# Where seven tiles begin in SBUF: the forms of x moved to seven places modulo 128 bytes

## The chip, the core and the metric

The kernel runs on one core of a Trainium2 chip. The metric is the device time of one execution in microseconds, lower is better. Three runs of the kernel before gave 974.46, 974.54 and 976.66 us (median 974.54 us).

## What is computed

The reference is attention with a block-causal mask over 4 batches, 8 heads, 576 positions and head size 64, followed by two layers of `x @ w_in`, a pointwise function, `@ w_out`, over 2304 tokens, with model width 512 and inner width 2048:

```python
attn = softmax(where(block_i >= block_j, q @ k.T / 8, -1e9)) ; x = attn @ v   # -> [2304, 512]
h = x @ w_in ; x = (h * cos(h)) @ w_out        # first layer
h = x @ w_in ; x = (max(h, 0) ** 2) @ w_out    # second layer, the output
```

All is float32. Each large product is made of three products of parts: a value is split into a high part that TensorE takes exactly in its fp32r format and a low part that is the rest, and `mm3` adds high·high, high·low and low·high in PSUM.

## The kernel before, in words

The order of the work on every engine is written out by a planner (`Recorder.schedule`) before the program is made. It works with costs, due times and data dependences of operations and knows nothing of addresses, so a change of addresses leaves its order as it is.

The first 400 us or so are attention and the first half of the first layer. The change touches what follows: three stages (`for stage in range(3)`, the second half of the first layer, and the two halves of the second one). Each stage goes over five groups of tokens (four of 512, one of 256). For a group of 512, x is cut into four quarters, and from these seven forms x0 to x6 are made: four quarters or sums of them, and three more sums, as in Strassen's scheme for 2x2 blocks (Winograd's variant). The seven forms of a half of `w_in` stand beside them in tiles named `w`, and `quad` multiplies form i of w with form i of x, in the order 0, 1, 5, 4, 6, 2, 3. One such product (`product`) is 12 matmuls: 2 halves of the output by 2 of the depth by the three of `mm3`. The weight part is the stationary operand (128 x 128, loaded by an LDWEIGHTS of its own), the part of x is the moving one, 256 columns wide. For the group of 256 tokens, `two` takes forms 0 and 1, then 0 and 4, 12 matmuls each. With two calls for each group and three stages, the matmuls into `h` that move a form of x are 24 x 12 = 288 for each form, plus 144 for x0 and 72 each for x1 and x4: 432 + 360 + 360 + 4 x 288 = 2304.

In the trace the matmul `h<-x,w` moves x and loads w; the buffer numbers are left out of names, so that all seven forms are called x. The LDWEIGHTS for the next matmul runs while a matmul moves its columns.

A form's tile is written by a copy of the high part (L472 on ScalarE) and a subtraction for the low part (L490 on VectorE) in the first two stages. In the second they are also sent to HBM (`xp_d<-x`), and in the third they are read back from there (`x<-xp_d`). In the third stage the product with `w_out` is done in seven forms too (`out_quad`, matmuls into `y`, 256 columns, the moving operand is a form of the weights, the stationary one a form of g). There the fourteen tiles of weight forms sit where room is: two in `raw` tiles, two in the `x` tiles (those that hold unsplit x in the earlier stages), one in `so` tiles, nine in `w` tiles.

**Where tiles begin.** A pool is a stretch of each partition of SBUF, taken in steps of 32 bytes, from the low end or (`side="right"`) from the high end, and its tiles follow each other in the order of their first use. From the sizes of pools and of the fill-in tiles between them (`shim`), counted in bytes modulo 128, the beginnings before the change are: all `w` tiles 0, in both of their pools; all of x, x0 to x6, and the `raw`, `so`, `g`, `c`, `t`, `n`, `ws` and `t0` to `t3` tiles 64. Parts inside a tile begin 512 or 1024 bytes or multiples of it further on, so each operand of a matmul begins where its tile does, modulo 128. A column is 4 bytes in each partition.

Of the kernel before, what the change touches and what calls it, by code (L numbers as in the profile page):

```python
# [11 lines left out]
F32R = mybir.dt.float32r  # L12
# [6 lines left out]
PSUM = bass.MemoryType.PSUM  # L19
# [37 lines left out]
class View:  # L57
    def __init__(self, vt, chain, ix, halves):
        self.vt, self.chain, self.ix, self.halves = vt, chain, ix, halves
# [34 lines left out]


class VTile(View):
    def __init__(self, pool, shape, dtype, tag, bufs, whole=False):
        self.pool, self.shape, self.dtype, self.tag, self.bufs = pool, shape, dtype, tag, bufs
        self.whole = whole
        n = int(np.prod(shape[1:]))  # L100
        self.grain = 32 if n >= 32 else 1
        self.full = (1 << (2 * (n // self.grain + 1))) - 1
        self.real = None
        self.users = []
        self.bank = self.banks = self.before = None
        super().__init__(self, [], np.arange(n).reshape(shape[1:]), 3)

    def alloc(self):
        if self.real is None:
            tag = self.tag if self.bank is None else f"bank{self.bank}"  # L110
            self.real = self.pool().tile(self.shape, self.dtype, tag=tag, name=self.tag, bufs=self.bufs)


class Banks:
# [30 lines left out]
class Recorder:  # L145
# [20 lines left out]
        self.kind = None  # L166
        self.phase = 0

    def tile(self, pool, shape, dtype, tag, bufs=1, whole=False):
        return VTile(pool, shape, dtype, tag, bufs, whole)  # L170

    @contextmanager
    def of(self, kind):
# [208 lines left out]
def kernel(  # L382
# [25 lines left out]
    R = Recorder()  # L408
# [172 lines left out]
    class Pool:  # L581


        def __init__(self, name, **kw):
            self.name, self.kw, self.pool, self.after, self.stack = name, kw, None, (), None
# [18 lines left out]
    def later(names, **kw):  # L604
        return [Pool(n, **kw) for n in names]
# [32 lines left out]
    xs_p, tmp = opened(s1, "xs1", "tmp1")  # L638
    (sb,) = opened(att, "att", side="right")

    def T(pool, shape, dtype, tag, bufs=1):
        return R.tile(pool, shape, dtype, tag, bufs, whole=pool.kw.get("space") == PSUM)

    x_d = T(dram, [KD, 128, NT], F32, "x_d")
    y1_d = T(dram, [KD, 128, NT], F32, "y1_d")
    y_d = T(dram, [KD, 128, NT], F32, "y_d")


# [27 lines left out]
    for i in range(2):  # L676
# [3 lines left out]
        whole = T(sb, [128, 128], F32, f"whole{i}")  # L680
# [585 lines left out]
    for group, steps in WORK:  # L1266
# [12 lines left out]
        if group == (3, 1):  # L1279
            wo_p, x3_p = later(("wo", "x3"), side="right")  # L1280
# [16 lines left out]
        return raw  # L1297

    def x_tile(j):
        return T(x3_p, [128, 2, 2, 256], F32R, f"x{j}")  # L1300

    def x_parts(forms, keep):

        ops = {}
        for j, x in forms:
            t = x_tile(j)
            hi, lo = t[:, 0], t[:, 1]
            hi_part(hi, x)
            lo_part(lo, x, hi)
            if keep is not None:  # L1310
                dma(keep[j], f(t).rearrange("p j k c -> p (j k c)"), 524288)
            ops[j] = hi, lo
        return ops

    @of("forms")
    def kept_parts(keep, which):

        ops = {}
        for j in which:
            t = x_tile(j)  # L1320
            dma(f(t).rearrange("p j k c -> p (j k c)"), keep[j], 524288)
            ops[j] = t[:, 0], t[:, 1]
        return ops
# [319 lines left out]
```

## Time and profile before

| | |
|---|---|
| median of three runs | 974.54 us |
| the profiled execution | 974.84 us, of it 973.0 us from its first to its last instruction |
| TensorE busy (matmuls) | 951.8 us, 98% of the span |
| VectorE, ScalarE, GpSimd busy | 713.8, 602.3, 208.3 us |
| matmuls `h<-x,w`, 128 x 256 | 2304 |

A busy time of TensorE is a union of intervals that overlap, since a matmul begins before the one before it has ended (one takes 276 ns from its first column to its last result, and begins some 115 ns after the one before). What a matmul costs is therefore read from the starts: the time from the start of one row to the start of the next in the timeline, divided by the matmuls in the row.

### The profile page before, as it was taken

To read this page: it belongs to the slowest core of one execution; us is meant where nothing else is said; L and a number is where in the kernel's file an instruction comes from. 1 tells how busy PE (TensorE), PEld (TensorE's weight loads), DVE (VectorE), ACT (ScalarE), POOL (GpSimd) and SP (SyncE) were. 2 spreads that over 40 slices of the span, in tenths; PEclk is the share of its full clock that TensorE was granted. 3 is DMA by queue.
4 is the path that set the end of the run, shared out by engine and by line. 5 is a ranking of instruction groups with operands and counts; after the bars stand their busy time and mean duration, and the time that the engine had idled before them with its cause. 6 is when DMAs were issued, how large, how long until landed. Compare 5 with 4: busy or idle time off the path is not lost.

```text
span 973.0 us, 19283 instructions
## 1 busy us (share of the span) xinstructions
PE 951.8 (98%) x6996; PEld 856.1 (88%) x6996; DVE 713.8 (73%) x1581; ACT 602.3 (62%) x1285; POOL 208.3 (21%) x313
## 2 busy tenths in 40 slices
PE   7979999999999999999999999999999999999998
PEld 5757987889898989999989889998898899999998
DVE  5898667687877455588879797987885737659565
ACT  5787588785889575484758476767564433324222
POOL 3554243447687781000000000000000000000000
PEclk8999999999999999999999999999999999999999
DMA  6755233355656347563355899796947779535321
GB/s 184 192 150 124 67 85 84 105 153 182 176 174 206 109 134 263 200 254 93 109 173 181 317 360 327 268 352 215 358 139 240 245 256 416 194 104 195 96 73 60
DMA packets 155150, 185.29 MB, mean 190 GB/s; under 512 B 71728, under 2 KB 119856, under 8 KB 155056
## 3 DMA queue, kind: packets, MB, share of 16 engines
q1 hardware_dynamic: 155056, 184.07, 57.5%
q8 instruction: 55, 0.90, 0.4%
q14 instruction: 39, 0.32, 0.1%
HBM read 114.29 MB, written 69.73 MB: 189 GB/s over the span
## 4 chain that ended last, share of the span: by engine, by line
PE 88%; DMA 5%; DVE 3%; ACT 2%; issue 1%; POOL 1%; SPq 0%; ACTq 0%; POOLq 0%; DVEq 0%
PE y L548 37%; PE h L548 34%; PE t L566 6%; PE a L558 5%; PE s L558 4%; DMA wi_d<-so 2%; PE s L548 1%; DMA x<-xp_d 1%; DMA w<-wf_d 1%; DMA x<-x_d 1%; DVE e L1046 1%; POOL e L531 0%; DVE c L449 0%; DVE c L748 0%; DVE so L490 0%
## 5 line engine op out<-in xcount | busy, mean ns | idle before, releaser
L548 PE MATMUL h<-x,w 128*128 128x256 f32 x2304 | 315.8, 278 | 1.7 <-DVE r L442 0.9
L548 PEld LDWEIGHTS h<-x,w 128*128 128x128 f32 x2304 | 294.4, 188 | 6.5 <-DVE r L442 1.7
L548 PE MATMUL y<-gh,w 128*128 128x256 f32 (+2 forms) x832 | 214.7, 329 | 7.3 <-POOL w L467 6.6
L548 PEld LDWEIGHTS y<-gh,w 128*128 128x128 f32 x832 | 144.3, 189 | 19.0 <-POOL w L467 7.6
L548 PE MATMUL y<-gl,w 128*128 128x256 f32 (+2 forms) x416 | 135.0, 328 | 0.0
L548 PE MATMUL y<-w,gh 128*128 128x512 f32 (+1 forms) x450 | 124.0, 354 | 0.4 <-DVE gh L490 0.4
L548 PEld LDWEIGHTS y<-w,gh 128*128 128x128 f32 x450 | 78.9, 188 | 12.6 <-DVE gh L490 0.6
L433 ACT ACTIVATE e<-e,st 128x256 f32<-128x256 f32 (+4 forms) x144 | 82.9, 577 | 8.6 <-DVE st L1046 6.9
L1046 DVE CUSTOM_DVE_ANT_0 e<-s,mask 128x128 f32<-128x128 f32 (+4 forms) x160 | 71.3, 478 | 22.9 <-PE s L558 15.3
L531 POOL TENSOR_SCALAR e<-e,st 128x256 f32<-128x256 f32 (+4 forms) x116 | 73.0, 640 | 63.0 <-DVE st L1067 37.0
L548 PEld LDWEIGHTS y<-gl,w 128*128 128x128 f32 x416 | 78.5, 189 | 6.2 <-issue 0.8
L548 PE MATMUL y<-w,gl 128*128 128x256 f32 (+1 forms) x306 | 83.5, 333 | 0.0
L472 ACT ACTIVATE gh<-r 128x512 fp32r<-128x512 f32 (+1 forms) x85 | 51.3, 610 | 40.0 <-DVE r L1404 18.2
L566 PE MATMUL t<-ident,e 128*128 128x128 f32 (+1 forms) x400 | 65.1, 282 | 4.6 <-DVE e L535 2.3
L490 DVE TENSOR_TENSOR gl<-r,gh 128x512 fp32r<-128x512 f32 (+1 forms) x83 | 54.7, 664 | 15.3 <-ACT gh L472 12.4
L442 DVE TENSOR_TENSOR o<-y,o 128x512 f32<-128x512 f32 (+1 forms) x55 | 34.8, 635 | 40.2 <-PE y L548 39.1
L548 PE MATMUL h<-xs2h,w 128*128 128x320 f32 x256 | 62.0, 313 | 0.0
L566 PEld LDWEIGHTS t<-ident,e 128*128 128x128 f32 (+1 forms) x400 | 46.4, 141 | 13.8 <-POOL e L531 4.7
L501 ACT ACTIVATE r<-t 128x384 f32<-128x384 f32 (+1 forms) x95 | 49.2, 531 | 14.6 <-PE t L566 13.1
L433 ACT ACTIVATE t<-raw,minus 128x512 int32<-128x512 int8 x64 | 48.8, 762 | 14.8 <-DMA raw<-in_moe_w_out_dram 6.8
L548 PEld LDWEIGHTS y<-w,gl 128*128 128x128 f32 x306 | 50.2, 188 | 6.1
L548 PE MATMUL h<-xs1h,w 128*128 128x256 f32 x256 | 53.5, 290 | 1.2 <-POOL w L467 0.7
(172 smaller groups left out, 1838.0 us busy)
## 6 DMA issues: line engine op xcount, KB each, us to landing
wi_d<-so SPq DMA_DIRECT2D x84, 256.0 KB, 2.8
w<-wi_d SPq DMA_DIRECT2D x42, 512.0 KB, 6.3
raw<-in_moe_w_in_dram SPq DMA_DIRECT2D x32, 512.0 KB, 4.6
raw<-in_moe_w_out_dram SPq DMA_DIRECT2D x32, 512.0 KB, 4.4
xp_d<-x SPq DMA_DIRECT2D x24, 512.0 KB, 6.0
x<-xp_d SPq DMA_DIRECT2D x24, 512.0 KB, 5.7
y_d<-o SPq DMA_DIRECT2D x34, 256.0 KB, 2.6
o<-y_d SPq DMA_DIRECT2D x32, 256.0 KB, 3.8
```

Source lines behind the costliest of these rows:

```text
L433: return nc.scalar.activation(real(out), real(in_), func, **kw)
L442: out.size / 0.96 + 68, lambda: nc.vector.tensor_tensor(real(out), real(a), real(b), op=op), [out], [a, b],
L472: "ACT": ("ACT", n / 1.2 + 92, lambda: nc.scalar.activation(real(hi), real(x), ACTF.Copy)),
L490: lambda: nc.vector.tensor_tensor(real(lo), real(x), real(f(hi)), op=ALU.subtract), 1,
L501: "ACT": ("ACT", n / 1.2 + 50, lambda: nc.scalar.activation(real(out), real(ps), ACTF.Copy)),
L531: lambda: nc.gpsimd.tensor_scalar(real(out), real(x), real(s), 1.0, op0=ALU.mult, op1=ALU.mult),
L548: lambda: nc.tensor.matmul(real(ps), lhsT=real(lhsT), rhs=real(rhs), start=start, stop=stop, skip_group_check=True),
L558: nc.tensor.matmul(real(ps), lhsT=real(l), rhs=real(r), start=start, stop=stop, skip_group_check=True)
L566: lambda: nc.tensor.transpose(real(out), real(in_), real(ident)[0:rows, 0:rows]), [out], [in_, ident],
L1046: lambda: nc.vector.tensor_tensor_reduce(out=real(e), in0=real(ps), in1=real(m), scale=-1.0, scalar=BIG, op0=ALU.add, op1=ALU.min, accum_o ...
```

## The change

A tile can be asked to lie in a larger slot, some elements behind its beginning. The seven tiles x0 to x6 (4096 bytes for each partition) get slots of 1032 elements, 4128 bytes, so that the beginnings step on by 32 bytes from one to the next, and x3, x5 and x6 begin 4 elements (16 bytes) behind their slot's beginning. The slots follow in the order of first use: x0, x1, x2, x4, x5, x6, x3. The pool grows by 7 x 32 = 224 bytes towards lower addresses, so that its two `x` tiles move as well. Nothing is issued more, less or in another order.

Beginnings modulo 128 bytes:

| tile | x0 | x1 | x2 | x3 | x4 | x5 | x6 | the two `x` tiles | `w` |
|---|---|---|---|---|---|---|---|---|---|
| before | 64 | 64 | 64 | 64 | 64 | 64 | 64 | 64 | 0 |
| after | 96 | 0 | 32 | 48 | 64 | 112 | 16 | 96 | 0 |

```diff
 class VTile(View):
-    def __init__(self, pool, shape, dtype, tag, bufs, whole=False):
+    def __init__(self, pool, shape, dtype, tag, bufs, whole=False, at=0, slot=0):
...
     def alloc(self):
         if self.real is None:
             tag = self.tag if self.bank is None else f"bank{self.bank}"
-            self.real = self.pool().tile(self.shape, self.dtype, tag=tag, name=self.tag, bufs=self.bufs)
+            if not self.slot_size:
+                self.real = self.pool().tile(self.shape, self.dtype, tag=tag, name=self.tag, bufs=self.bufs)
+                return
+
+            t = self.pool().tile([self.shape[0], self.slot_size], self.dtype, tag=tag, name=self.tag, bufs=self.bufs)
+            t = t[:, self.at:self.at + int(np.prod(self.shape[1:]))]
+            names = "abc"[:len(self.shape) - 1]
+            sizes = dict(zip(names, self.shape[1:]))
+            self.real = t.rearrange(f"p ({' '.join(names)}) -> p {' '.join(names)}", **sizes) if len(names) > 1 else t
...
     def x_tile(j):
-        return T(x3_p, [128, 2, 2, 256], F32R, f"x{j}")
+        return T(x3_p, [128, 2, 2, 256], F32R, f"x{j}", at=4 * (j in (3, 5, 6)), slot=1032)
```

## Rows read from the trace of the kernel before

**Rows 1.** The page: busy time of engines, the clock, and the chain's shares.
```profile
PE 951.8 (98%) x6996; PEld 856.1 (88%) x6996; DVE 713.8 (73%) x1581; ACT 602.3 (62%) x1285; POOL 208.3 (21%) x313
...
PEclk8999999999999999999999999999999999999999
...
PE 88%; DMA 5%; DVE 3%; ACT 2%; issue 1%; POOL 1%; SPq 0%; ACTq 0%; POOLq 0%; DVEq 0%
PE y L548 37%; PE h L548 34%; PE t L566 6%; PE a L558 5%; PE s L558 4%; DMA wi_d<-so 2%; PE s L548 1%; DMA x<-xp_d 1%; DMA w<-wf_d 1%; DMA x<-x_d 1%; DVE e L1046 1%; POOL e L531 0%; DVE c L449 0%; DVE c L748 0%; DVE so L490 0%
```

**Rows 2.** Waits of PE from 405 to 960 us: total, times, longest.
```profile
PE h L548 <- DVE r L442: 0.9, 2, 0.6
PE h L548 <- ACT p L501: 0.4, 1, 0.4
PE y L548 <- ACT gh L472: 0.4, 1, 0.4
PE h L548 <- DMA x<-xp_d: 0.2, 1, 0.2
PE h L548 <- DMA w<-wi_d: 0.2, 1, 0.2
```

**Rows 3.** PE's timeline: start, us, then what; long runs of h.
```profile
706.55 15.17 PE L548 MATMUL h<-x,w 128*128 128x256 f32 x132
721.55 0.62 PE L548 MATMUL y<-w,gh 128*128 128x512 f32 x2
...
723.18 3.69 PE L548 MATMUL h<-x,w 128*128 128x256 f32 x30
726.71 0.39 PE L548 MATMUL y<-w,gh 128*128 128x512 f32 x1
```

**Rows 4.** The chain from 411 us: first and last of 29 pieces `PE h` with 20 or more.
```profile
414.02 4.73 PE h L548 x40
...
953.53 5.42 PE h L548 x46
```

**Rows 5.** PE's timeline in the last stage, runs of y.
```profile
855.47 0.64 PE L548 MATMUL y<-x,gl 128*128 128x256 f32 x4
855.95 0.88 PE L548 MATMUL y<-x,t 128*128 128x256 f32 x6
856.67 0.88 PE L548 MATMUL y<-x,gl 128*128 128x256 f32 x6
857.39 0.64 PE L548 MATMUL y<-w,gh 128*128 128x256 f32 x4
857.86 0.84 PE L548 MATMUL y<-w,c 128*128 128x256 f32 x6
858.54 0.84 PE L548 MATMUL y<-w,gh 128*128 128x256 f32 x6
859.22 0.39 PE L548 MATMUL y<-so,c 128*128 128x256 f32 x2
```

**Rows 6.** PE's timeline, single h between single y: first, one stretch, last of 155.
```profile
824.88 0.28 PE L548 MATMUL h<-x,w 128*128 128x256 f32 x1
...
865.82 0.28 PE L548 MATMUL y<-w,gh 128*128 128x256 f32 x1
865.94 0.28 PE L548 MATMUL h<-x,w 128*128 128x256 f32 x1
...
867.24 0.77 PE L548 MATMUL y<-w,gl 128*128 128x256 f32 x5
...
953.13 0.28 PE L548 MATMUL h<-x,w 128*128 128x256 f32 x1
```

**Rows 7.** Instructions that touch tiles named x: count, ns min/median/max.
```profile
L548 PE MATMUL h<-x,w x2304: 274/276/388, 405.4 to 958.7; 128*128 128x256 f32 x192
L548 PE MATMUL y<-x,t x54: 278/283/288, 813.0 to 960.8; 128*128 128x256 f32 x54
L548 PE MATMUL y<-x,gl x54: 274/283/283, 813.7 to 962.4; 128*128 128x256 f32 x54
L472 ACT ACTIVATE x<-t x34: 615/622/637, 408.8 to 729.5; 128x512 fp32r<-128x512 f32 x34
L490 DVE TENSOR_TENSOR x<-t,x x34: 681/685/692, 412.5 to 730.3; 128x512 fp32r<-128x512 f32 x34
L573 SPq DMA_DIRECT2D x<-xp_d x24: 319/320/528, 811.4 to 923.9; - x24
DMA to landing us min/median/max: 2.7/5.7/10.9
```

More of the change, by code (lines that the diff above doesn't have):

```diff
@@ L96 @@
 class VTile(View):
-    def __init__(self, pool, shape, dtype, tag, bufs, whole=False):
+    def __init__(self, pool, shape, dtype, tag, bufs, whole=False, at=0, slot=0):
         self.pool, self.shape, self.dtype, self.tag, self.bufs = pool, shape, dtype, tag, bufs
-        self.whole = whole
+        self.whole, self.at, self.slot_size = whole, at, slot
         n = int(np.prod(shape[1:]))
@@ L167, in __init__, with tile @@
         self.phase = 0
-    def tile(self, pool, shape, dtype, tag, bufs=1, whole=False):
-        return VTile(pool, shape, dtype, tag, bufs, whole)
+    def tile(self, pool, shape, dtype, tag, bufs=1, whole=False, at=0, slot=0):
+        return VTile(pool, shape, dtype, tag, bufs, whole, at, slot)
     @contextmanager
@@ L639, with T @@
     (sb,) = opened(att, "att", side="right")
-    def T(pool, shape, dtype, tag, bufs=1):
-        return R.tile(pool, shape, dtype, tag, bufs, whole=pool.kw.get("space") == PSUM)
+    def T(pool, shape, dtype, tag, bufs=1, at=0, slot=0):
+        return R.tile(pool, shape, dtype, tag, bufs, pool.kw.get("space") == PSUM, at, slot)
     x_d = T(dram, [KD, 128, NT], F32, "x_d")
```

## The prediction

> **What bounds the kernel.** The page's busy times come first: TensorE is at work for 98% of the span, the other engines for 73% and less, and the chain that ended last runs 71% of its time over the matmuls into y and h [rows 1]. The clock row shows full speed, 2.4 GHz, from the second of forty slices on [rows 1]. Then TensorE's waits in the part that uses the forms of x: they sum to 2.1 us in 555 [rows 2]. So the only question is how fast the matmuls follow each other, and for that the timeline is read from start to start.
>
> **What the trace says of places.** In the kernel before every `h<-x,w` moves an operand at 64 beside weights at 0 (modulo 128 bytes, as everywhere below), 64 bytes apart. The longest run begins its 132 matmuls in 721.55 - 706.55 = 15.00 us, 113.6 ns each. But another run with the same places takes (726.71 - 723.18) / 30 = 117.7 ns [rows 3]: at one distance there are two paces, and a run keeps the one it fell into. Over all 29 longer pieces of h on the chain, from 413 us on, the mean is 162.68 us / 1419 = 114.6 ns [rows 4].
>
> The trace has one other distance. In the last stage the two weight forms in `x` tiles move from 64 while the stationary g, at 64 too, is loaded: distance 0. These 16 matmuls of 256 columns take (857.39 - 855.47) / 16 = 120.0 ns. Right behind them weights in `w` tiles, at 0, move beside g at 64, distance 64 again: twelve in 859.22 - 857.86 = 1.36 us, 113.3 ns; the four in between take 0.47 us, 117.5 ns each [rows 5]. Nothing but the place of the moving operand differs between the two halves. So I take distance 0 to cost 120.0 - 114.6 = 5.4 ns for each matmul more than distance 64, and a change of distance some 4 x (117.5 - 113.3) = 17 ns until the pace is there.
>
> The Trainium skill says otherwise: TensorE: Matmul & The Clock Gate, Part 2 (step by step, loading the stationary operand), has it that loading the next tile's weights takes no SBUF read bandwidth from the running matmul, since the two go through read ports of their own. By that rule places would not count and the time would stay at 974.5 us. The trace does not agree, by 120.0 against 113.3 ns above; the rule stays as a rival below.
>
> **The change part by part.** *Forms of x against w.* New distances to 0, taken the shorter way round: x0 32, x1 0, x2 32, x3 48, x4 64, x5 16, x6 16. Only 0 and 64 are in the trace. Between them I take a straight line, the plainest thing between two points: 5.4 ns x (64 - d) / 64. Times the counts (432, 360, 360 for x0, x1, x4, 288 for each of the others, 2304 in all [rows 7]): x0 1.17, x1 1.94, x2 0.78, x3 0.39, x4 0, x5 1.17, x6 1.17 us, in all +6.6 us. Bounds: if only distance 0 costs, x1 alone loses, +1.9 us. If each distance but 64 costs the full 5.4 ns, 1944 matmuls lose 10.5 us. Below nothing: the faster of the two paces seen at 64 is 113.3 ns, and if all forms but x1 fell into it, that were 1944 x 1.3 = -2.5 us, -0.6 with x1. A pace below 113.3 stands in no row for 256 columns; it is a rival.
>
> *Single h between single y in the last stage.* 155 of the 2304 are alone between two matmuls of y [rows 6]. The load that runs beside them is that of g, at 64, so that they are at distance 0 now: twelve of such a stretch take 867.24 - 865.82 = 1.42 us, 118.3 ns each. The new distances to 64 have a mean near 34. They leave the sum above with 155 / 2304 x 6.6 = 0.45 us, and gain 155 x 3.7 x 34 / 64 = 0.3 us: -0.75 us, between 0 and -1.
>
> *Two weight forms in the last stage.* The two `x` tiles go from 64 to 96, from distance 0 to 32 beside g; 108 matmuls [rows 7] gain half of 5.4 ns: -0.3 us, bounds 0 and -0.7.
>
> *Borders between forms.* Now a quad runs through its seven forms at one distance. Afterwards each of 24 x 7 = 168 borders is a change of distance. Price 0 to 17 ns each, 0 to 2.9 us. As some steps are small I take half, +1.4 us.
>
> *Writers and DMAs.* The copies and subtractions that write the forms (622 and 685 ns) and the reloads (5.7 us to landing) [rows 7] write to places that are no longer multiples of 64. No row shows such a write. TensorE waits for a reload once, 0.2 us, and for none of these copies [rows 2], so that ordinary growth of them lies beside matmuls: 0, with up to +1 us if the 24 reloads take a fifth longer and the first of the stage, on the chain, shows it.
>
> **Sum.** 6.6 - 0.75 - 0.3 + 1.4 = +7.0 us on the profiled execution's 974.84 us: 981.8. That execution lies 0.3 us above the median of the runs shown, 974.54, so I say 981.5 us. Since TensorE is slowed on its own, nothing behind it becomes late; its waits can only shrink, by 2.1 us at most.
>
> **Rivals.** (a) *The pace goes by distance in one direction.* At 2.4 GHz 256 columns are 106.7 ns; the rows are 6.7 and 13.3 ns over that, 16 and 32 columns, and 64 bytes are 16 columns. So the next matmul may begin only when the moving operand's place comes round again: a surplus of distance / 4 columns, 0 standing for 32. Against 113.3 x0 at 96 is then +3.3 ns, x1 +6.7, x2 -3.3, x3 -1.7, x5 +5.0, and x6 +8.3 or -5.0 (whether 4 columns are enough is not known): 1.44 + 2.40 - 0.96 - 0.48 + 1.44 and +2.40 or -1.44 give +6.2 or +2.4 us; the other direction gives the same two. 977 to 981 us. For it: the round numbers. Against it: the pace of 117.7 ns at the same distance.
>
> (b) *Places hardly count.* Either only distance 0 costs, 974.54 + 1.9 = 976.4, or none does: 974.5. For it: two paces at one distance [rows 3], so something else sets the pace also. Against it: the pace turns at a border, with the place alone [rows 5]. (The second of the two is what the quoted page of the Trainium skill would make of the change.)
>
> (c) *Not slower: places off the multiples of 64 are better than both.* x0, x2, x3, x5 and x6 make 1584 matmuls. If their pace falls as far below 114.6 as distance 0 lies above it, to 109.2, that gives -8.6 us; with x1's +1.9 and the -0.3 of the weights, -7.0: 967.5 us. The kernel becomes faster from a mean below 114.6 - 1.9 / 1.584 = 113.4 ns for the five, and by over 0.3% from 111.6 ns. For it: no row shows those places, and 113.3 is still 6.7 ns over the bare columns. Against it: no run of the trace is below 113.3.
>
> (d) *The slots don't step as meant*, if the 16 bytes were lost in rounding: x5 at 96, x6 at 0, x3 at 32 cost 0.78 + 1.56 + 0.78 = 3.1 us against 2.7; within the forecast.
>
> **Chances.** The forecast's line, with borders dearer or cheaper, 978 to 988 us: 0.5. (a) 0.2. (b) 0.18. (c) 0.12. A difference under 0.3%, 2.9 us, can't be told from none here. Faster by more is two thirds of (c), 0.08. Within it: most of (b), the rest of (c) and a fifth of (a), 0.24. Slower: 0.68. The range leaves out (c), the lower part of (b), and what lies above the dearest sum, 974.54 + 10.5 + 2.9 = 988: 974.0 to 988.5 us. The likeliest case alone is 978 to 988.
>
> **What would show it.** Runs of twelve matmuls in a quad, in the order x0, x1, x5, x4, x6, x2, x3, should no longer have one pace: x4 near 113.3 to 114.6, x1 near 120, x5 and x6 near 118.7, x0 and x2 near 117, x3 near 116, with a step of a few matmuls at each border; the long row of 132 should take about 15.5 us. The `y<-x` runs should fall from 120.0 towards 117. If all twelves keep 113.3 or 117.7 it is (b); if x2 and x0 lie on different sides of 113.3 it is (a); if the twelves of x0, x2, x3 lie under 112 it is (c). Longer waits of TensorE, or a ratio of run to pace that the twelves don't explain, would make the whole sum wrong.

## The result, and the profile after

The changed kernel takes 980.48 us in the median of four runs (979.23 to 981.39), against 974.50 us before: a ratio of 1.0062, 95% interval [1.0049, 1.0075]. It is slower by 6 us; 981.5 us was forecast.

The profiled execution took 979.23 us, its span is 977.3 us. First the page, the lines that answer to [rows 1].

```profile
PE 956.7 (98%) x6996; PEld 862.4 (88%) x6996; DVE 713.6 (73%) x1581; ACT 602.5 (62%) x1285; POOL 208.6 (21%) x313
...
PE 90%; DMA 3%; DVE 3%; ACT 2%; POOL 1%; issue 1%; ACTq 0%; POOLq 0%; SPq 0%; DVEq 0%
```

TensorE is busy 4.9 us longer, and no other engine is by more than 0.3. Its waits in the part that uses the forms (404 to 965 us), which answer to [rows 2]:

```profile
PE h L556 <- ACT p L509: 0.2, 1, 0.2
PE h L556 <- DVE r L450: 0.2, 1, 0.2
```

They have gone from 2.1 to 0.4 us: a slower TensorE finds its operands ready. What it lost is in the pace. TensorE's timeline, the two runs that answer to [rows 3] (lines of the program are eight further on):

```profile
708.84 15.74 PE L556 MATMUL h<-x,w 128*128 128x256 f32 x132
724.41 0.62 PE L556 MATMUL y<-w,gh 128*128 128x512 f32 x2
...
726.04 3.71 PE L556 MATMUL h<-x,w 128*128 128x256 f32 x30
729.58 0.40 PE L556 MATMUL y<-w,gh 128*128 128x512 f32 x1
```

The same 132 matmuls take 724.41 - 708.84 = 15.57 us, 118.0 ns each, where it was 113.6. The thirty, which were slow before at 117.7 ns, are as slow now, 118.0. On the chain there are 31 pieces of h with 20 or more matmuls; first and last, against [rows 4]:

```profile
413.28 13.21 PE h L556 x112
...
957.88 5.48 PE h L556 x46
```

Together 189.53 us for 1602, 118.3 ns; before it was 114.6. The runs of y in the last stage, against [rows 5]:

```profile
859.29 0.86 PE L556 MATMUL y<-x,t 128*128 128x256 f32 x6
860.00 0.86 PE L556 MATMUL y<-x,gl 128*128 128x256 f32 x6
860.70 0.63 PE L556 MATMUL y<-w,gh 128*128 128x256 f32 x4
```

`y<-x`, whose weights went from distance 0 to 32, has (860.70 - 859.29) / 12 = 117.5 ns, 120.0 before. And what touches x otherwise, against [rows 7], is as it was, the copies at places off 64 too:

```profile
L480 ACT ACTIVATE x<-t x34: 615/622/634, 408.0 to 732.4; 128x512 fp32r<-128x512 f32 x34
L498 DVE TENSOR_TENSOR x<-t,x x34: 681/686/694, 411.7 to 733.2; 128x512 fp32r<-128x512 f32 x34
```

From every matmul's start to the next one's, those that begin with a wait (140 ns and over) left out, the matmuls into h have a mean of 114.97 ns before (2294 of them) and 118.13 ns after (2301): 3.16 x 2300 = +7.3 us, and the waits give 1.7 us back. (The two profiled executions lie 4.4 us apart and not 6: in the new one the part ahead of the first `h<-x,w` was 0.8 us shorter, 404.6 us against 405.4.) By form, inside runs of h:

| | x0 | x1 | x2 | x3 | x4 | x5 | x6 |
|---|---|---|---|---|---|---|---|
| distance after | 32 | 0 | 32 | 48 | 64 | 16 | 16 |
| ns before | 114.9 | 114.5 | 114.7 | 114.7 | 114.6 | 114.1 | 114.9 |
| ns after | 118.9 | 118.9 | 117.7 | 118.8 | 117.0 | 117.7 | 117.9 |
| rise | 4.0 | 4.4 | 3.0 | 4.1 | 2.4 | 3.6 | 3.0 |
| rise forecast | 2.7 | 5.4 | 2.7 | 1.35 | 0 | 4.05 | 4.05 |

The total was right and the shape was not: all forms rose by 2.4 to 4.4 ns, and x4, which did not move modulo 128, lost 2.4 ns: its matmuls of 114 ns or less fell from 73% to 20%. This is what the experiments are about.

### The profile page after: what moved, and what is told of

The parts are those of the page before. It is cut to its first block, busy times and chain, and to the rows that moved or that the text cites. A ratio compares the mean times of both kernels' runs of the same rounds, so it can differ in the third digit from the quotient of the medians.

```text
span 977.3 us, 19283 instructions
## 1 busy us (share of the span) xinstructions
PE 956.7 (98%) x6996; PEld 862.4 (88%) x6996; DVE 713.6 (73%) x1581; ACT 602.5 (62%) x1285; POOL 208.6 (21%) x313
## 4 chain that ended last, share of the span: by engine, by line
PE 90%; DMA 3%; DVE 3%; ACT 2%; POOL 1%; issue 1%; ACTq 0%; POOLq 0%; SPq 0%; DVEq 0%
PE y L556 38%; PE h L556 36%; PE t L574 6%; PE a L566 5%; PE s L566 4%; DMA wi_d<-so 2%; PE s L556 1%; DMA xp_d<-x 1%; DMA raw<-in_moe_w_in_dram 1%; DVE e L1054 0%; POOL e L539 0%; DVE c L756 0%; DVE c L457 0%; ACT r L441 0%; ACT c L441 0%
## 5 line engine op out<-in xcount | busy, mean ns | idle before, releaser
L556 PE MATMUL h<-x,w 128*128 128x256 f32 x2304 | 322.6, 281 | 0.4 <-ACT p L509 0.2
L556 PEld LDWEIGHTS h<-x,w 128*128 128x128 f32 x2304 | 300.9, 188 | 4.6 <-DVE r L450 0.6
```

Source lines behind the costliest of these rows:

```text
L556: lambda: nc.tensor.matmul(real(ps), lhsT=real(lhsT), rhs=real(rhs), start=start, stop=stop, skip_group_check=True),
```

## The experiments

Names of theories, as in the expectations: L, the prediction's straight line in the distance; F, 64 has a fast pace and no other distance does; M, only changes of distance cost; P, a run keeps the pace that it fell into, and a form at another place throws it out of the fast one; S, it is steps between the places of forms and hardly the places themselves; R and A, relative or absolute place. Each kernel ran on the same chip as the kernel before; the ratio is to its runs there. In the table "h" is the mean from start to start of all h matmuls without waits, in one profile of each kernel, "of 132" the pace of the run shown above.

| kernel | places of x0 to x6 modulo 128 | slots, bytes | ratio, 95% interval | h, ns | of 132, ns |
|---|---|---|---|---|---|
| before | 64 | 4096 | 1 | 114.97 | 113.6 |
| step256 | 64 | 4096 and 4352 | 1.0001 [0.9988, 1.0013] | 114.85 | 113.7 |
| swap | 0, all w at 64 | 4096 | 1.0000 [0.9991, 1.0009] | 114.93 | 113.7 |
| aim | 64 | 4096 | 1.0006 [0.9995, 1.0018] | 115.07 | 113.6 |
| one128 | 64, x1 a step of 128 aside | 4096, x1 4352 | 1.0035 [1.0022, 1.0048] | 116.46 | 115.4 |
| all64 | 64 | 4224 | 1.0047 [1.0032, 1.0061] | 117.03 | 117.4 |
| one0 | 64, x1 at 0 | 4224 | 1.0048 [1.0029, 1.0066] | 117.23 | 117.8 |
| all32 | 32 | 4224 | 1.0048 [1.0029, 1.0067] | 117.82 | 117.7 |
| uni32 | 32 | 4096 | 1.0053 [1.0035, 1.0071] | 117.35 | 117.3 |
| all48 | 48 | 4224 | 1.0064 [1.0045, 1.0083] | 118.42 | 118.6 |
| all0 | 0 | 4224 | 1.0076 [1.0056, 1.0096] | 118.78 | 118.9 |
| uni0 | 0 | 4096 | 1.0081 [1.0062, 1.0099] | 119.02 | 119.2 |
| all72 | 72 | 4224 | 1.0106 [1.0093, 1.0119] | 120.05 | 120.5 |

**One distance for all forms.** Line 1308 of the changed kernel, everything else as there:

```diff
-        return T(x3_p, [128, 2, 2, 256], F32R, f"x{j}", at=4 * (j in (3, 5, 6)), slot=1032)
+        return T(x3_p, [128, 2, 2, 256], F32R, f"x{j}", at=28, slot=1056)              # all48
+        return T(x3_p, [128, 2, 2, 256], F32R, f"x{j}", at=24, slot=1056)              # all32
+        return T(x3_p, [128, 2, 2, 256], F32R, f"x{j}", at=16, slot=1056)              # all0
+        return T(x3_p, [128, 2, 2, 256], F32R, f"x{j}", at=16 * (j == 1), slot=1056)   # one0
```

all48: 

> All seven forms of x begin at 48, 48 bytes from the weights at 0; nothing else moves. Theory L (the line of the prediction: the pace goes by the distance alone, 114.6 ns at 64, 120.0 at 0, straight between): 1.35 ns more for 2304 matmuls, +3 us, no borders to pay, about 977.5 us. Theory F (flat: 64 is one special distance, each other one has about the pace that the changed kernel shows for it, 119.3 ns at 48): 4.5 x 2304 = +10 us, 985 us. Theory M (only the change of distance between forms costs, one distance throughout is as good as another unless it is 0): 974.5 us and runs at 113.3 ns.

all32: 

> All seven forms of x at 32. L: 2.7 ns x 2304 = +6.2 us, 980.7 us, runs at 117.3 ns. F: the changed kernel's runs of x2 at 32 have 116.8 ns in the mean, with a pattern of 113 to 120 that comes again every four matmuls: +5 us, 979.5 us. M: 974.5 us, runs at 113.3 ns. L and F lie close here; the pattern within a run is what is looked at.

all0: 

> All seven forms of x at 0, the place of the weights. L: 5.4 ns x 2304 = +12.4 us, 987 us, less some 0.7 us for the single h of the last stage, which are then 64 from g. F: the changed kernel's runs of x1 at 0 have 118.8 ns: +9.7 us, 984 us; if they settle at the 120.0 ns of the y runs when nothing disturbs them, 987 us. M: it is the one distance that costs in itself, 987 us. What a mean of 118 would say is that a run at 0 does not settle.

one0: 

> Only x1 begins at 0, the other six stay at 64. L: 5.4 ns x 360 = +1.9 us and 48 borders at 0 to 17 ns, up to +0.8: 976.4 to 977.2 us; the forms at 64 keep their mean of 114.6 ns. Theory P (a run keeps the pace that it falls into, and a form at another distance throws it out of the fast one): the forms behind x1 in a quad (x5, x4, x6, x2, x3) run at 117.8 ns more often than before; if all six did always, 1944 x 3.2 = +6.2 us more, 982 us. In the changed kernel x4 at 64 ran at 116.9 ns in the mean.

all48 took 980.29 us against 974.08, and its long run 15.66 us:

```profile
709.34 15.82 PE L556 MATMUL h<-x,w 128*128 128x256 f32 x132
725.00 0.63 PE L556 MATMUL y<-w,gh 128*128 128x512 f32 x2
```

all32 took 978.83, all0 981.67, one0 978.56 us. L falls with all48, which should have been the cheapest of the three that move all forms (977.5) and is dearer than all32, 118.42 ns against 117.82; M seems to fall too, with no run at 113.3 in any of them. F comes nearest, but only for all32 (979.5) does its time fit: it gave 985 for all48 and 984 to 987 for all0, 5 and 2 us too much at least. (The paces that it takes for x3 and x2, 119.3 and 116.8 ns, are not those of the whole trace in the table above, 118.8 and 117.7.) one0 seemed to show P: one form of seven costs almost what all seven cost, and the six at 64 had 116.4 to 117.1 ns. But these four share something beside the places, the slots of 4224 bytes.

**The slots alone.** All forms at 64 in such slots, and 8 bytes off that place:

```diff
-        return T(x3_p, [128, 2, 2, 256], F32R, f"x{j}", at=4 * (j in (3, 5, 6)), slot=1032)
+        return T(x3_p, [128, 2, 2, 256], F32R, f"x{j}", at=0, slot=1056)   # all64
+        return T(x3_p, [128, 2, 2, 256], F32R, f"x{j}", at=2, slot=1056)   # all72
```

all64: 

> All seven forms at 64 as before, but in slots of 4224 bytes, so that the larger pool and the longer steps between the tiles are there and the places are not changed. If the places are all there is to it: 974 us and a mean of 115 ns; if the larger slots or the moved pool cost something themselves: up to 979 us.

all72: 

> All seven forms at 72, 8 bytes off the good place, distance 56. Theory L: 0.7 ns x 2304 = +1.6 us, 975.7 us. Theory F in its sharp form (the fast pace of 113.3 ns exists at 64 alone): no run at 113.3, a mean of 117 to 118.5 ns, +5 to +8 us, 979 to 982 us. Theory F in a wide form (it exists within 8 bytes): 974 us.

The control was no control. With every place modulo 128 as before, all64 took 978.53 us against 974.18, and both runs of the timeline have the slow pace, (724.50 - 709.00) / 132 = 117.4 ns and 118.0 ns:

```profile
709.00 15.66 PE L556 MATMUL h<-x,w 128*128 128x256 f32 x132
724.50 0.63 PE L556 MATMUL y<-w,gh 128*128 128x512 f32 x2
...
726.13 3.70 PE L556 MATMUL h<-x,w 128*128 128x256 f32 x30
729.67 0.39 PE L556 MATMUL y<-w,gh 128*128 128x512 f32 x1
```

4224 is 33 x 128, so that neighbouring forms lie 128 apart modulo 256. The weights in `w` lie at 0 modulo 256 in one of their pools and at 128 in the other, so that both 64 and 192 occur as distances modulo 256, in the kernel before too. Sorted by the distance modulo 256 from the moving operand to the weights that are loaded beside it, 2% of 1000 matmuls at 64 are at 114 ns or less, and 42% of 935 at 192. In the kernel before 64 alone had 69%, and 192 had 74%. So the distance is not the whole of it: what a run does depends on how it came there. In the trace of the kernel before, of the stretches of nine and more matmuls of one form at 64, all 60 that begin fast (their second to fourth at 114.2 ns or less in the mean) end fast (so the last three before the last) and all 28 that begin slow end slow; at 192 all 43 that begin fast end fast, and of 20 that begin slow 10 end fast. one0 differs from all64 by x1's place only, and the two take the same time: its loss came from the slots, and my reading of it as P was not yet earned. all72 is the slowest of all, 984.80 us, 120.05 ns:

```profile
712.41 16.06 PE L556 MATMUL h<-x,w 128*128 128x256 f32 x132
728.31 0.63 PE L556 MATMUL y<-w,gh 128*128 128x512 f32 x2
```

That is nearest to F in the sharp form, for the place 8 bytes off 64 has no run at 113.3. But F gave at most 982 us and 118.5 ns; all72 is dearer still than distance 0 in the same slots (all0), where L had +1.6 us. 72 is also the one place tried that is no multiple of 16 bytes; whether its cost comes from that or from the distance was not tried.

**Relative or absolute, and the weights of the last stage.** From the kernel before (aim from the changed one's `VTile`, with its forms of x put back):

```diff
-    shim(ctx, "shim1", 32)                          # swap
+    shim(ctx, "shim1", 96)
-    shim(ctx, "shim3", 96, side="right")
+    shim(ctx, "shim3", 32, side="right")
...
-        return T(x3_p, [128, 2, 2, 256], F32R, f"x{j}", at=4 * (j in (3, 5, 6)), slot=1032)   # aim
+        return T(x3_p, [128, 2, 2, 256], F32R, f"x{j}")
-                    got[c][i] = [T(pool, [128, 2, 256], F32R, tag, n) for _ in "hl"]
+                    got[c][i] = [T(pool, [128, 2, 256], F32R, tag, n, at=16, slot=544) for _ in "hl"]
-                    t = T(pool, [128, 2, 2, 256], F32R, tag, n)
+                    aside = {"raw": dict(at=16, slot=1056), "x": dict(at=16, slot=1056)}.get(tag, {})
+                    t = T(pool, [128, 2, 2, 256], F32R, tag, n, **aside)
```

swap: 

> The kernel before with every pool moved on by 64 bytes: all w tiles at 64, x0 to x6, raw, so, g and the rest at 0. All distances between x, w, g stay 64 where they were 64. Theory R (the distance between the moving part and the weights being loaded counts): as before, 974 us, runs of h at 113.3 or 117.8 with a mean near 115 ns. Theory A (the moving operand's own place counts, 64 being the good one): 118.8 ns as with all forms at 0, 981 to 982 us.

aim: 

> The kernel before with the forms of w_out that lie in raw, x and so tiles in the last stage moved to 0, 64 from g, where they were at distance 0; x0 to x6 stay at 64. 270 matmuls of y then have distance 64. By the rows of before (119 ns against 116) they gain about 0.8 us. By theory P, that a form at distance 0 also throws the following ones out of the fast pace, the other y matmuls of 256 columns of the last stage gain too (mean 117.5 ns now): up to 750 x 2.5 ns = 1.9 us. 972 to 973.5 us, near what can be measured.

swap took 974.68 us against 974.18, and its long run is that of the kernel before:

```profile
704.98 15.17 PE L548 MATMUL h<-x,w 128*128 128x256 f32 x132
719.99 0.62 PE L548 MATMUL y<-w,gh 128*128 128x512 f32 x2
```

R, the relative place. aim gave nothing, 974.13 us, ratio 1.0006 [0.9995, 1.0018]: the mean of the 256-column y matmuls did not fall (117.4 ns against 117.3), a miss of my expectation. The moved forms did gain, those in `raw` from 118.9 to 116.4 ns and those in `x` from 119.3 to 117.5 (those in `so` did not, 118.1 and 118.0); but the 480 that move weights in `w`, which had stayed where they were, lost, from 116.5 to 117.6, which made up for it. Single h and y matmuls still alternate there at distance 0 and break up runs; that this is the reason was not tried.

**Steps against places, with the slots set right.** From the kernel before (uni) and the changed one:

```diff
-                    shim(stack, "shim4", 64, side="right")
+                    shim(stack, "shim4", 128, side="right")     # uni0
+                    shim(stack, "shim4", 96, side="right")      # uni32
...
-        return T(x3_p, [128, 2, 2, 256], F32R, f"x{j}", at=4 * (j in (3, 5, 6)), slot=1032)
+        return T(x3_p, [128, 2, 2, 256], F32R, f"x{j}", slot=1088 if j in (1, 2, 4, 5, 6) else 1024)   # step256
+        return T(x3_p, [128, 2, 2, 256], F32R, f"x{j}", at=32 * (j == 1), slot=1088 if j == 1 else 1024)   # one128
```

uni0: 

> All of x3 moved on by 64 bytes with the slots of 4096 bytes of the kernel before: x0 to x6 (and the two x tiles) all at 0 and a whole number of 4096 bytes apart. Theory S (what costs is that the forms no longer lie at one place modulo 256 or more, so that a run changes its address relation at each border and loses the fast pace; the place modulo 128 itself costs little): 974.5 us, runs at 113.3 ns. Theory F (distance 0 has no fast pace of its own): 118.8 to 120.0 ns, +9 to +12 us, 983 to 986 us.

uni32: 

> The same with all of x3 at 32. Theory S: 974.5 us and runs at 113.3 ns. Theory F: 117.1 to 118.2 ns as with all forms at 32 in slots of 4224 bytes, 979 us. In between: a pace at 32 that is steady without borders, but over 113.3.

step256: 

> All forms of x at 64, five of the seven in slots of 4352 bytes, so that the steps between them are 4096 or 4352 bytes: one place modulo 256, several modulo 4096. If the place modulo 256 decides, as the two halves of the run with slots of 4224 suggest (distance 192 modulo 256 fast in 4 of 10 matmuls, 64 in 2 of 100): 974.2 us, a mean of 115 ns. If each step other than 4096 bytes costs: 978.5 us, 117 ns.

one128: 

> Only x1 is moved by 128 bytes, so that it stays 64 from the weights modulo 128 and is the one form at another place modulo 256. Theory P (a run keeps the pace it fell into): the five forms behind x1 in a quad lose the fast pace in the quads where it leaves them at 64 modulo 256, 976.5 to 978.5 us. If only x1's own twelve matmuls change their pace: 288 + 72 matmuls by up to 3 ns, at most +1 us, 975.2 us.

step256 took 973.66 us against 973.73: steps of 4352 bytes cost nothing.

```profile
706.74 15.18 PE L556 MATMUL h<-x,w 128*128 128x256 f32 x132
721.75 0.62 PE L556 MATMUL y<-w,gh 128*128 128x512 f32 x2
```

one128 took 977.47 us: one form, 128 bytes aside and still 64 from the weights modulo 128, costs 3.7 us.

```profile
709.50 15.39 PE L556 MATMUL h<-x,w 128*128 128x256 f32 x132
724.73 0.63 PE L556 MATMUL y<-w,gh 128*128 128x512 f32 x2
```

Inside these 132 the quad's second form, x1, is at 117.8 ns in both quads. In the first one x5 behind it is back at 113.3 ns from its fourth matmul; there its distance is 192 modulo 256. In the second one x5 and x4 stay at 117.8; there it is 64. Over the whole trace x5, x4, x6, x2 and x3 have 1 to 18% at 114 ns or less where they lie at 64, and 48 to 80% at 192. x1 itself has 1 and 6%. So P holds: x1's 360 matmuls alone, at 3.2 ns, make 1.2 us, and the rest is what it leaves to its followers. It is a step of the moving operand that does it, not one of the distance: where a run goes on from weights in one pool to weights in the other, the distance goes from 192 to 64 modulo 256, and in the kernel before all 10 stretches that follow a fast one there stay fast. After a step of 128 bytes of the moving operand none of 15 does in one128, and none of 18 in all64.

uni0 and uni32 took 981.79 and 979.09 us against 973.73: no step from form to form modulo 256, and no run at 113.3. uni0 first, then uni32:

```profile
711.55 15.89 PE L548 MATMUL h<-x,w 128*128 128x256 f32 x132
727.28 0.63 PE L548 MATMUL y<-w,gh 128*128 128x512 f32 x2
...
708.27 15.65 PE L548 MATMUL h<-x,w 128*128 128x256 f32 x132
723.76 0.62 PE L548 MATMUL y<-w,gh 128*128 128x512 f32 x2
```

(uni0: 15.73 us, 119.2 ns. In its second quad, at 0 modulo 256, x1 and x5 go at 120 ns matmul for matmul, the pace of `y<-x` in [rows 5]; in the first one, at 128, 115, 117, 122, 120 and 119 come again and again.) S alone falls. F stands in its order, with 979 us right for uni32 and 983 to 986 somewhat high for uni0. Of the places tried, a long run holds 113.3 ns only where two conditions are met: a distance of 64, and no step of 128 bytes modulo 256 from form to form. Breaking the second alone costs 4.4 us (all64), breaking the first alone 5.4 and 8.1 (uni32, uni0), and breaking both no more than that, 4.8 and 7.6 (all32, all0): the two losses do not add up. How the 6 us of the changed kernel divide between its places and its steps no run separates.

Two other readings are answered by the traces. uni0 also moved x against whatever the other engines use; but its matmuls inside runs of h take 119.4 ns where VectorE is busy all the while and 118.9 where it is idle (ScalarE: 119.3 and 119.2), and in the kernel before 114.6 with VectorE busy or idle. One product of 12 in uni0's long run takes 1.42 us where the DMA engines are at 0.48 of their time (712.98 to 714.40 us), and another takes the same where they are at 0.00 (715.83 to 717.25). And it is the weights being loaded that count, not those in use: the 155 single h of [rows 6] use `w` while g is loaded, and in uni0, where x is 0 from `w` and 64 from g, they are faster than before, 116.5 ns against 118.4, and so is `y<-x`, 116.6 against 119.3.

## Why the prediction was right, and where it was wrong

*The total.* +7.0 us was forecast, +6.0 came. That it came out so near was in part luck: errors in the terms below cancelled each other.

*What bounds.* Right. With the h slower by 3.2 ns in the mean the kernel became slower by nearly the sum of it; the waits of TensorE gave back 1.7 us, where I had said 2.1 at most and entered nothing.

*Distance 0 costs 5.4 ns.* The sign was right, the size a third too high. uni0 is the clean measurement: 119.02 - 114.97 = 4.05 ns over all h, +8 us, where the prediction's line gives 12.4 us for all forms there. 120.0 ns is a pace that such a run settles to at times, not its mean.

*The straight line.* Wrong, and this is the step that failed: "a straight line, the plainest thing between two points". uni32 costs 2.4 ns, not far from the line's 2.7; but all48 with 118.42 ns is dearer than all32 with 117.82 in the same slots, and all72, 8 bytes off the good place, is dearest. Over all64, which has these slots and the good distance, all32 costs 0.8 ns, all48 1.4, all0 1.75 and all72 3.0; that is no line. There is no slope towards 64, there is one good distance among those tried. The forecasts of 1.35 ns for x3 and 0 for x4 are the victims (4.1 and 2.4 measured), and that for x0 (4.0 where 2.7 was forecast); those for x1, x5 and x6 were too high, and the errors cancelled: +6.6 us were entered.

*Borders, 0 to 17 ns each, +1.4 us taken.* The mechanism was taken from [rows 5], where a pace came back after four matmuls, and its upper bound of 2.9 us was too low: all64, which has nothing but steps modulo 256, costs 4.4 us. Its places modulo 128 are unmoved, so that by the prediction's reckoning it has no change of distance at all. A border does not cost its own few matmuls, it puts the whole next form into the slow pace. The trace of before had shown the two paces, at one distance in [rows 3], and the prediction even says that a run keeps the one it fell into; but then it reckons with a mean of 114.6 instead of asking what throws a run from one into the other.

*Single h and the two weight forms.* The 155 single h of [rows 6] went from 118.4 to 118.1 ns, 0.05 us where a gain of 0.3 was forecast. `y<-x` fell from 119.3 to 117.4 ns over its 108, -1.9 where -2.7 was forecast.

*Writers and DMAs at 0.* Right as far as seen: the copies have the medians of before in the rows above, TensorE's waits have not grown, and step256, whose pool is larger than the changed kernel's, costs nothing.

*The rivals.* (a) wanted x2 and x3 under 113.3 ns; no form of any kernel has a mean there. (c) falls with it. (b) falls by uni0 and uni32: distances do count, with no instruction changed and the one pool moved. With it goes the rule quoted from the Trainium skill (TensorE: Matmul & The Clock Gate, Part 2, step by step): uni0 issues the same instructions as before and differs by 64 bytes, at 1.0081 [1.0062, 1.0099]. What inside the chip ties the two streams together was not shown by any run.

## What to carry to other kernels

Where TensorE is the bound and matmuls are short, read their pace from start to start and see whether one shape has two paces; here 113.3 and 117.8 ns for the same instruction made the 4.4 us of all64. Put the moving operand and the weights loaded beside it at a distance that the trace shows to be fast (64 bytes here, and by swap only the difference counts), and keep moving operands that follow one another at one place modulo 256: tiles padded by 128 bytes cost 4.4 us here, not much less than a distance of 32 (uni32, 5.4). And a control that changes only the padding belongs to every experiment on places; without all64 I would have taken one0 for a proof.

## What was not expected of the hardware

At 64 modulo 256 from the weights a run of matmuls has two paces that both last: 113.3 ns, kept for the last 47 of the 132 of the kernel before (the first 85 lie at 192), and 117.8 ns, kept for its 30. It comes into the second by one form at another place (x1 in one128), and from it hardly returns at distance 64 (2% of the matmuls in all64 are fast), but often does at 192 (42%). Eight bytes off the fast place (all72, 120.05 ns) were worse than 64 bytes off in the same slots (all0, 118.78). None of the thirteen variants was faster than the kernel before.
